# A message-passing layer on one core: groups of small units are formed in two periods instead of four or more, the first with 16 tiles instead of 48

## The chip, the cores and the metric

The kernel runs on one core of a Trainium2 chip. The metric is the device time of one execution in microseconds; the span in a profile, from the first to the last instruction, is a little shorter. Engines are named as in the profile: PE multiplies matrices, DVE and ACT work element by element, POOL issues the indirect transfers (gathers and scatters by a list of indices), SP issues the plain ones.

## The reference

A graph has 12500 nodes with 64 features and 800000 edges with 16 attributes, a source and a destination each. Every edge gets a message from both its nodes' features and its attributes; the messages are summed at their destination, and the nodes are updated:

```python
m_in = jnp.concatenate([x[src], x[dst], e_attr], axis=-1)
msg = _silu(m_in @ w_msg)
agg = _segment_sum(msg, dst, N)
return _silu(jnp.concatenate([x, agg], axis=-1) @ w_upd)
```

Sources and destinations are drawn at random, so the edges come in no order.

## The kernel before, in words

**What is computed where.** The product of the concatenation with the weights is split. `tables` (L214) computes each node's part as a source into a table in HBM, `A_d`, and its part as a destination into `BW`, kept on the chip. Of an edge there is then left: take the row of its source from the table, add the part of its destination and of its attributes, apply silu, and add the result to the sum of its destination. Destinations lie in 128 buckets of 98 nodes. Within a tile of 128 edges that all belong to one bucket, destinations can be handled as a one-hot matrix of 98 columns, by products on PE.

**Two halves.** The first half sorts edges into buckets, in a store `st` in HBM; the second takes sorted tiles from the store and computes messages. Both run interleaved.

The first half works in *steps* of 8 tiles (`class Step`, L377; 782 of them). `onehot` (ACT, L394 and L395) marks each edge's bucket, `sums` (L397) and `count` (PE, L421 to L424) count the edges of each bucket, `ranks` (DVE, L429) finds each edge's place in its bucket, `expand` (DVE, L442) puts its record (16 attributes, and source and destination in one number) at that place, `move` (PE, L459) brings the records to their bucket's row. After 8 or 12 tiles the row block is copied (ACT, L464), the buckets' pointers are advanced (`place`, L477 and L478), and POOL scatters the block to the store (`scatter`, L482). The first 140 chunks have 8 tiles, so nearly every one of these steps scatters; later chunks have 12, so two steps in three do. The steps read segments of indices (`seg_load`, 9 steps each) and edge attributes (`ea_load`, L243, 3 steps each) by plain transfers that SP issues; `records` (ACT at L272) reads the attributes one period after they were asked for.

The second half works in *batches* of up to 8 tiles (`class Batch`, L616): `gather` (POOL, L645, one instruction for each tile), `onehot` (DVE at L655, ACT at L656), `transpose` (PE at L664, ACT at L667), `product` (PE, L673), `message` (DVE at L677, ACT at L678), `reduce` (PE, L694), `add` (DVE, L706). There are 818 batches with 6322 gathers.

**Groups.** Batches belong to *groups* (`class Group`, L489). A group is a list of units of `u` tiles that are taken from the buckets as far as these are filled. The kernel begins with units of one tile (64 tiles in all, in batches of 8), goes on with units of two (640 tiles in groups of 24 and batches of 6), and then has units of four in groups of 64 (`FIRST`, L37, and `QU`). Forming a group takes several stages, numbered by `g.k`, one for each period:

- 0: *bounds*. Five small DVE operations (L540 to L545) count each bucket's new units, a product on PE with a triangular matrix (L577) sums them up over the buckets. Its result lies in the PSUM buffer with the tag `ag`, which `reduce` uses too; there is one such buffer.
- 1: *matrix*. Nine DVE operations (L548 to L558) make from it a matrix that says which unit comes from which bucket; three products on PE (L581 to L583) turn it into a list.
- 2 and on: *loads*. DVE writes the list as integers (`rows`, L588 and L589), SP reads it and issues one transfer for each unit (L564) from the store to one of four buffers `rt`. `NL` (L39) says how many a period has: 16 units of one tile, 8 of two, 8 of four. The transfers wait for the last scatter that was issued when the bounds were computed (L570).
- `g.t0`: *indices*. DVE converts the sources to integers, `sidx` (L525), and the destinations to `lo` (L526, L527). Only two groups may be past this point and not yet used up.

`g.t0` is 2 plus the number of periods with loads. After stage `t0` the group is ready, and the next period may take its first batch.

**The order.** It is written out by hand: `period` (L711) emits, for every engine, one piece of each stage of both halves. Each engine executes its own instructions strictly in this order. A step passes through its stages in successive periods (one-hot and sums; count, ranks and expansion; move; scatter), and so does a batch: gather in the first, transposes and product in the second, message in the third, reduction and addition in the fourth. Formation stages come in two places: `fourth` (DVE) near the start of the period, behind the batch's one-hot, and `middle` (PE) and `fifth` (DVE) at its end.

**The planner.** Whether a group may start is decided when the program is built, without the data. `Draws` (L768) fills 16 sets of buckets with random numbers of a fixed seed, and a group starts when all 16 hold enough (`holds`, L799), when the stage has tiles left (`size`, L817), and when no other group is at an earlier stage of its formation (`may_start`, L852). So the program, and with it the period in which each group starts, is fixed. `step` (L858) is one period with a step; 782 of them are followed by the periods that empty the store.

Of the kernel before, what the change touches and what calls it, by code (L numbers as in the profile page):

```python
# [3 lines left out]
F32 = mybir.dt.float32  # L4
# [3 lines left out]
OP = mybir.AluOpType  # L8
# [6 lines left out]
P = 128  # L15
NBK = 128
BK = 98
# [5 lines left out]
M = 8  # L23
# [3 lines left out]
S = LIM[-1]  # L27
# [6 lines left out]
QU = 4  # L34
# [1 line left out]

FIRST = [(1, 48, BT, (1, 0, 1, 0)), (2, 24, 6, (3, 3, 2, 2))]  # L37
DUM = GT
NL = {1: 16, 2: 8, QU: 8}  # L39
ZB = M // 2  # L40
RK = float(C * P)
SEG = 9 * M
# [6 lines left out]
def mpnn_kernel(tc, x, e_attr, src, dst, w_msg, w_upd, out):  # L49
    nc = tc.nc  # L50
# [22 lines left out]
    with es:  # L73
# [46 lines left out]


        cb = pc.tile([P, 512], F32, name="cb")
        ioB = cb[:, 0:P]
        ioS = cb[:, P:P + S]
        hit = cb[:, 2 * P:2 * P + M * S].rearrange("p (k s) -> p k s", s=S)
        nc.vector.tensor_copy(ioB, iof)
        nc.vector.tensor_scalar(out=ioS, in0=iof[:, 0:S], scalar1=RK, scalar2=None, op0=OP.add)


# [359 lines left out]
        class Group:  # L489


            def __init__(g, u, ptr, done_old, done_new, ceil, gt=GT, base=None, cap=None, bt=BT):
                g.u, g.ptr, g.done_old, g.done_new, g.ceil, g.gt = u, ptr, done_old, done_new, ceil, gt
                g.base = ub[u] if base is None else base
                g.b0, g.cap = None, cap
                g.gu, g.bt = gt // u, bt
                g.nl = NL[u]
                g.t0 = 2 + (g.gu + g.nl - 1) // g.nl
                g.k = 0
                g.over = False  # L500
                g.rt = RT[state["rt"]]
                state["rt"] = (state["rt"] + 1) % len(RT)
# [27 lines left out]
            def fourth(g):  # L530
                k = g.k
                gu = g.gu
                if k == 0:
                    urec = g.u * P
                    c = (urec - 1) / (2.0 * urec) * (1.0 if g.ceil else -1.0)
                    g.blocks = len(blocks)
                    wl = wp.tile([NBK, 8], F32, name="wl")
                    g.wl = [wl[:, i:i + 1] for i in range(8)]
                    a1, v, new, e0, s, e, t1, cbc = g.wl
                    nc.vector.scalar_tensor_tensor(out=a1, in0=g.ptr, scalar=1.0 / urec, in1=g.base, op0=OP.mult, op1=OP.subtract)  # L540
                    nc.vector.tensor_scalar(out=v, in0=a1, scalar1=c, scalar2=MAGIC, op0=OP.add, op1=OP.add)
                    if g.cap is not None:
                        nc.vector.tensor_tensor(out=v, in0=v, in1=g.cap, op=OP.min)
                    nc.vector.scalar_tensor_tensor(out=new, in0=v, scalar=-MAGIC, in1=g.done_old, op0=OP.add, op1=OP.subtract)
                    nc.vector.tensor_tensor(out=t1, in0=g.base, in1=g.done_old, op=OP.add)  # L545
                elif k == 1:
                    a1, v, new, e0, s, e, t1, cbc = g.wl
                    nc.vector.tensor_tensor(out=e0, in0=g.ps[:, 0:1], in1=new, op=OP.add)  # L548
                    nc.vector.tensor_scalar(out=s, in0=g.ps[:, 0:1], scalar1=float(gu), scalar2=None, op0=OP.min)  # L549
                    nc.vector.tensor_scalar(out=e, in0=e0, scalar1=float(gu), scalar2=None, op0=OP.min)  # L550
                    g.mat = mat = wp.tile([NBK, GT], F32, name="mat")
                    nc.vector.tensor_scalar(out=mat[:, 0:gu], in0=iof[:, 0:gu], scalar1=s, scalar2=None, op0=OP.is_ge)

                    nc.vector.tensor_tensor(out=t1, in0=t1, in1=s, op=OP.subtract)
                    nc.vector.tensor_tensor(out=a1, in0=e, in1=s, op=OP.subtract)
                    nc.vector.scalar_tensor_tensor(out=mat[:, 0:gu], in0=iof[:, 0:gu], scalar=e, in1=mat[:, 0:gu], op0=OP.is_lt, op1=OP.mult)
                    nc.vector.tensor_scalar(out=cbc, in0=t1, scalar1=float(g.u), scalar2=-float(D0), op0=OP.mult, op1=OP.add)
                    nc.vector.tensor_tensor(out=g.done_new, in0=g.done_old, in1=a1, op=OP.add)  # L558
                elif k < g.t0:
                    if k == 2:  # L560
                        g.rows()
                    for u in range((k - 2) * g.nl, min(gu, (k - 1) * g.nl), 8):
                        for i, t in enumerate(regs(g.row, u, min(8, gu - u), ENG.SP, TOP - g.u)):
                            j = nc.sync.dma_start(g.rt[:, (u + i) * g.u:(u + i + 1) * g.u, :].rearrange("p a c -> p (a c)"),  # L564
                                                  st_t[ds(t, g.u), :].rearrange("t (q f) -> (t q) f", f=g.u * R))
                            tc.add_to_no_dep_group("units", j.ins)
                            if len(blocks) > g.blocks:
                                for b in blocks[g.blocks:]:
                                    tc.declare_no_dep(j.ins, b, reason=WHOLE)
                                tc.add_manual_dep(j.ins, blocks[g.blocks - 1].name, mybir.DependencyInfo(mybir.DependencyClass.Sync, mybir.DependencyReason.DATA), reason=WHOLE)  # L570

            def middle(g):

                gu = g.gu
                if g.k == 0:
                    g.ps = pag.tile([P, 512], F32, name="ps1", tag="ag")
                    nc.tensor.matmul(g.ps[:, 0:1], tri, g.wl[2], start=True, stop=True)  # L577
                elif g.k == 1:
                    cbc, mat = g.wl[7], g.mat
                    g.ps = pag.tile([P, 512], F32, name="ps2", tag="ag")  # L580
# [35 lines left out]
        class Batch:  # L616
# [35 lines left out]
            def onehot(t):  # L652
                i0, n = t.i0, t.n
                t.q = qp.tile([P, BT, KQ], F32, name="q")
                nc.vector.tensor_tensor(out=t.q[:, 0:n, 0:BK], in0=ioB[:, None, 0:BK].to_broadcast([P, n, BK]), in1=t.grp.lo[:, i0:i0 + n, None].to_broadcast([P, n, BK]), op=OP.is_equal)  # L655
# [55 lines left out]
        def period(step=None, batch=None, ptr_new=None):  # L711
# [17 lines left out]
                g.fourth()  # L729
            if z:  # L730
                z.count()
            if t:
                t.transpose(0)
                t.weights()
                t.transpose(1)
# [12 lines left out]
                z.expand()  # L748
            if h and not early:
                h.sums()  # L750
            if p:
                e = p.move(0)
            if t:
# [62 lines left out]

        def size():  # L817
            g = stages[state["stage"]]
            return g["gt"] if g["total"] is None else min(g["gt"], g["total"] - state["taken"])

        work = dict(cur=None, forming=[], b=0, used=0)

# [35 lines left out]
        def step():  # L858
# [5 lines left out]
            if pipe["z"] and pipe["z"].last:  # L864
                if flow["npl"] % 64 == 0:
                    flow["ptrs"] = sg.tile([NBK, 64], I32, name="ptrs")
                pn = flow["ptrs"][:, flow["npl"] % 64:flow["npl"] % 64 + 1]
                flow["npl"] += 1
            b = take()
            if size() and may_start() and draws.holds(state["u"], size() // state["u"]):  # L870
                draws.take(state["u"], size() // state["u"])
# [11 lines left out]
            next(tab)  # L883
        while flow["ic"] < len(steps) or pipe["h"] or pipe["z"]:
            step()
            for _ in range(4 if flow["ic"] < 5 else 1):
                next(tab, None)
            if zeros and flow["ic"] > 1:
                later()
# [285 lines left out]
```

## Time and profile before

| what | us |
|---|---|
| median of three runs | 8929.77 |
| lowest and highest | 8925.74 and 8931.5 |
| the profiled execution | 8929.85 |
| its span, first to last instruction | 8928.0 |
| last gather issued | 8906.46 |

The page of the profile gives each engine's busy time with its share of the span; a group of instructions has a line, an engine, an operation, the tile that it writes and those that it reads, the number, the busy time and mean duration, and the idle time of the engine just before them with what ended it. In the timeline the first column is the start and the second the duration, both in us; brackets at the end hold the idle time of the engine before the instruction, and who ended it. SPq and POOLq are the queues of an engine that issues transfers.

### The profile page before, as it was taken

The page shows a single profiled execution, that of the slowest core. Times are in us where ns is not written, and L with a number is a line of the kernel's source. Part 1 is how long each engine was busy: PE and PEld are TensorE (multiplying, and loading weights), DVE is VectorE, ACT ScalarE, POOL GpSimd, SP SyncE. Part 2 cuts the span into 40 slices and gives each one's busy share as a digit, 9 for nine tenths or more (in the row PEclk, how much of TensorE's full clock was granted, in tenths as well). Part 3 has the DMA queues.
Part 4 walks back from the last instruction along what each step waited for, and adds up shares of the span by engine and source line. Part 5 has one row for each costly group of instructions (what it writes and reads, how often), then busy time and mean ns, then how long its engine had stood idle before and what let it go on. Part 6 is the DMA issues. An engine that isn't in the chain of part 4 may idle for free. (4 is left out here: it accounts for less than half of the span.)

```text
span 8928.0 us, 155380 instructions
## 1 busy us (share of the span) xinstructions
PE 8156.2 (91%) x49053; PEld 5873.2 (66%) x49816; DVE 7216.6 (81%) x15722; ACT 5054.3 (57%) x12594; POOL 6599.6 (74%) x6908
## 2 busy tenths in 40 slices
PE   8899999999999999999999999999999999999767
PEld 5677776666666666666666666666666666666656
DVE  8999998888888888888888888888888888887233
ACT  7666666555555555555555555555555555555222
POOL 1677777777777777777777777777777777777776
PEclk9999999999999999999999999999999999999566
DMA  4222222222222222222222222222222222222323
GB/s 109 56 62 60 60 61 58 50 57 54 54 56 50 57 52 56 52 56 52 56 52 56 56 52 52 55 57 52 56 52 56 52 56 55 52 57 49 59 48 51
DMA packets 662901, 501.14 MB, mean 56 GB/s; under 512 B 492983, under 2 KB 529911, under 8 KB 662071
## 3 DMA queue, kind: packets, MB, share of 16 engines
q0 software_dynamic: 238976, 349.72, 16.8%
q1 hardware_dynamic: 422775, 141.27, 7.3%
q8 instruction: 401, 6.57, 0.3%
q14 instruction: 429, 3.51, 0.1%
q10 hardware_dynamic: 320, 0.07, 0.0%
HBM read 330.05 MB, written 152.30 MB: 54 GB/s over the span
## 5 line engine op out<-in xcount | busy, mean ns | idle before, releaser
L645 POOL DMA_INDIRECT g<-A_d,sidx x6322 | 6020.1, 952 | 1946.6 <-issue 1546.2
L459 PE MATMUL pl<-X,hf 128*128 128x291 f32 (+5 forms) x12512 | 4255.3, 492 | 6.2 <-DVE LOST L477 6.2
L459 PEld LDWEIGHTS pl<-X,hf 128*128 128x128 f32 x12512 | 2389.5, 198 | 1333.1 <-issue 842.5
L442 DVE TENSOR_TENSOR X<-cb,rec 128x442 f32<-128x442 f32 (+5 forms) x3128 | 2646.9, 908 | 26.7
L394 ACT ACTIVATE hf<-iof,shi 128x128 f32<-128x128 f32 x6256 | 1908.3, 389 | 872.9 <-PE pl L459 872.6
L673 PEld LDWEIGHTS pre<-w,qt 114*128 114x128 f32 x10496 | 1338.1, 202 | 580.7 <-issue 562.8
L673 PE MATMUL pre<-w,qt 114*128 114x64 f32 x10496 | 1343.6, 284 | 249.0 <-DVE g L677 247.3
L677 DVE TENSOR_TENSOR g<-pre,g 128x512 f32<-128x512 f32 (+1 forms) x818 | 548.9, 671 | 1191.7 <-DMA g<-A_d,sidx 769.4
L678 ACT ACTIVATE g<-g 128x512 f32<-128x512 f32 (+1 forms) x818 | 501.6, 613 | 1761.5 <-DVE g L677 1759.7
L694 PE MATMUL ag<-q,g 128*64 128x98 f32 x12644 | 775.8, 264 | 250.4 <-DVE wl L549 146.1
L429 DVE TENSOR_REDUCE rank<-z 128x8 f32<-128x1024 f32 x782 | 949.1, 1214 | 57.3 <-PE z L424 36.3
L395 ACT ACTIVATE hf<-hf,ones 128x1024 f32<-128x1024 f32 x782 | 899.1, 1150 | 25.4
L667 ACT ACTIVATE qt<-tq 114x1024 f32<-114x1024 f32 (+1 forms) x818 | 797.2, 975 | 156.5 <-PE tq L664 154.2
L664 PE MATMUL tq<-ident,q 128*114 128x128 f32 x6322 | 871.5, 283 | 14.3 <-ACT nodes L194 13.0
L694 PEld LDWEIGHTS ag<-q,g 128*64 128x64 f32 x12644 | 613.3, 143 | 411.5 <-issue 200.6
L664 PEld LDWEIGHTS tq<-ident,q 128*114 128x114 f32 x6322 | 766.9, 140 | 136.5 <-ACT nodes L194 20.5
L482 POOL DMA_INDIRECT st<-blk,ptrs x567 | 572.9, 1010 | 321.2 <-issue 141.1
L655 DVE TENSOR_TENSOR q<-cb,lo 128x784 f32<-128x784 f32 (+1 forms) x818 | 767.4, 938 | 2.2
L464 ACT ACTIVATE blk<-pl 128x512 f32<-128x512 f32 (+1 forms) x568 | 323.8, 570 | 782.9 <-PE pl L459 609.7
L706 DVE TENSOR_TENSOR ACC<-ag,ACC 64x98 f32 x1938 | 497.5, 257 | 108.6 <-PE ag L694 28.8
L422 PE MATMUL z<-G,onesb 128*128 128x384 bf16 x1564 | 511.4, 327 | 73.5 <-DVE G L403 13.7
L673 PE MATMUL pre<-BW,qt 114*128 (+1 forms) x2148 | 311.8, 305 | 109.4 <-DVE g L677 108.6
(137 smaller groups left out, 5099.1 us busy)
## 6 DMA issues: line engine op xcount, KB each, us to landing
g<-A_d,sidx POOLq DMA_INDIRECT x6322
ea<-in_e_attr SPq DMA_DIRECT2D x260, 192.0 KB
rt<-st SPq DMA_DIRECT2D x1312, 34.0 KB
st<-blk,ptrs POOLq DMA_INDIRECT x567
rt<-st SPq DMA_DIRECT2D x434, 8.5 KB
nodes<-in_x SPq DMA_DIRECT2D x62, 98.0 KB
ACC<-rt SPq DMA_DIRECT2D x11, 544.0 KB
rt<-st SPq DMA_DIRECT2D x320, 17.0 KB
```

Source lines behind the costliest of these rows:

```text
L394: nc.scalar.activation(c.hf[:, k, :], iof, AF.Square, bias=c.hi[:, k:k + 1])
L395: nc.scalar.activation(c.hf, c.hf, AF.Relu, bias=ones, scale=-1.0)
L429: nc.vector.tensor_reduce(out=c.rank, in_=c.z, axis=AX.X, op=OP.max)
L442: nc.vector.tensor_tensor(out=c.x[:, k:k + 2, 2:2 + n * R].rearrange("p k (s c) -> p k s c", c=R), in0=hit[:, k:k + 2, 0:n, None].to_broad ...
L459: nc.tensor.matmul(pl[:, 0:w], c.hf[:, k, :], c.x[:, k, 0:w], start=(n == (c.size - 1 if whole else 0)), stop=ends, skip_group_check=True)
L482: i = nc.gpsimd.indirect_dma_start(out=st, out_offset=bass.IndirectOffsetOnAxis(ap=c.ptr, axis=0), in_=c.blk[:, 2:], in_offset=None)
L645: j = nc.gpsimd.indirect_dma_start(out=t.g[:, i, :], out_offset=None, in_=A_d, in_offset=bass.IndirectOffsetOnAxis(ap=t.grp.sidx[:, k:k + ...
L655: nc.vector.tensor_tensor(out=t.q[:, 0:n, 0:BK], in0=ioB[:, None, 0:BK].to_broadcast([P, n, BK]), in1=t.grp.lo[:, i0:i0 + n, None].to_broa ...
L664: nc.tensor.transpose(t.tq[0:KQ, j * P:(j + 1) * P], t.q[:, j, :], ident)
L667: nc.scalar.activation(t.qt[:, 0:w], t.tq[0:KQ, 0:w], AF.Copy)
L673: nc.tensor.matmul(t.pre[:, i * D:(i + 1) * D], t.qt[:, i * P:(i + 1) * P], w, start=True, stop=True)
L694: o = nc.tensor.matmul(t.ag[t.half(v), v // 2 * BK:(v // 2 + 1) * BK], t.g[:, i, :], t.q[:, i, 0:BK], start=(k == 0), stop=(k == u - 1))
```

## The change

Four things change.

- **Formation of groups of one- and two-tile units** (those with a cap, `quick`). Bounds and matrix fall into one period: the product of the bounds is emitted right behind `count`, the matrix behind `expand` and `sums`, its three products at the period's end. All loads fall into the next period: `NL[2]` becomes 12, and `g.nl` is the whole group. `g.t0` still counts the periods by `NL`, 16 units each for one-tile units: 3 for the first group and for groups of two-tile units, 5 for the group of 48. The indices are made at the beginning of the period that follows, ahead of `take`, so that this same period can take the first batch.
- **The first group** has 16 tiles instead of 48; the second has the other 48.
- **The bounds' product** is written to one column of the constants' PSUM buffer `cb`, for every group, no longer to the buffer that `reduce` uses. The constants are narrowed for it.
- **The tables** are advanced twice in every fourth period instead of once in each.

Groups of four-tile units keep their stages.

```diff
-NL = {1: 16, 2: 8, QU: 8}
+NL = {1: 16, 2: 12, QU: 8}
...
-        ioB = cb[:, 0:P]
-        ioS = cb[:, P:P + S]
-        hit = cb[:, 2 * P:2 * P + M * S].rearrange("p (k s) -> p k s", s=S)
-        nc.vector.tensor_copy(ioB, iof)
+        ioB = cb[:, 0:BK]
+        ioS = cb[:, BK:BK + S]
+        hit = cb[:, P:P + M * S].rearrange("p (k s) -> p k s", s=S)
+        nc.vector.tensor_copy(ioB, iof[:, 0:BK])
+        ps1 = cb[:, 2 * P + M * S:2 * P + M * S + 1]
...
-                g.nl = NL[u]
-                g.t0 = 2 + (g.gu + g.nl - 1) // g.nl
+                g.quick = cap is not None
+                g.nl = g.gu if g.quick else NL[u]
+                g.t0 = 2 + (g.gu + NL[u] - 1) // NL[u]
...
-                    nc.vector.tensor_tensor(out=e0, in0=g.ps[:, 0:1], in1=new, op=OP.add)
-                    nc.vector.tensor_scalar(out=s, in0=g.ps[:, 0:1], scalar1=float(gu), scalar2=None, op0=OP.min)
+                    nc.vector.tensor_tensor(out=e0, in0=ps1, in1=new, op=OP.add)
+                    nc.vector.tensor_scalar(out=s, in0=ps1, scalar1=float(gu), scalar2=None, op0=OP.min)
...
-                    g.ps = pag.tile([P, 512], F32, name="ps1", tag="ag")
-                    nc.tensor.matmul(g.ps[:, 0:1], tri, g.wl[2], start=True, stop=True)
+                    nc.tensor.matmul(ps1, tri, g.wl[2], start=True, stop=True)
...
             if z:
                 z.count()
+            quick = [g for g in forms if g.quick and g.k == 0]
+            for g in quick:
+                g.middle()
+                g.k = 1
...
             if h and not early:
                 h.sums()
+            for g in quick:
+                g.fourth()
...
-            return g["gt"] if g["total"] is None else min(g["gt"], g["total"] - state["taken"])
+            if g["total"] is None:
+                return g["gt"]
+            return NL[1] if not state["stage"] and not state["taken"] else min(g["gt"], g["total"] - state["taken"])
...
+            for g in work["forming"]:
+                if g.quick and g.k == g.t0:
+                    g.fifth()
             b = take()
...
-            for _ in range(4 if flow["ic"] < 5 else 1):
+            for _ in range(4 if flow["ic"] < 5 else 1 + (flow["ic"] % 4 == 1)):
                 next(tab, None)
```

More of the change, by code (lines that the diff above doesn't have):

```diff
@@ L654, in onehot @@
                 t.q = qp.tile([P, BT, KQ], F32, name="q")
-                nc.vector.tensor_tensor(out=t.q[:, 0:n, 0:BK], in0=ioB[:, None, 0:BK].to_broadcast([P, n, BK]), in1=t.grp.lo[:, i0:i0 + n, None].to_broadcast([P, n, BK]), op=OP.is_equal)
+                nc.vector.tensor_tensor(out=t.q[:, 0:n, 0:BK], in0=ioB[:, None, :].to_broadcast([P, n, BK]), in1=t.grp.lo[:, i0:i0 + n, None].to_broadcast([P, n, BK]), op=OP.is_equal)
                 nc.scalar.activation(t.q[:, 0:n, BK:KQ], t.grp.rt[:, i0:i0 + n, 0:DE], AF.Copy)
```

## The prediction

> **What bounds the kernel now.** I read the page's busy line, then the groups and waits of POOL alone, then the timeline around the first batches, the only place with holes.
>
> ```profile
> PE 8156.2 (91%) x49053; PEld 5873.2 (66%) x49816; DVE 7216.6 (81%) x15722; ACT 5054.3 (57%) x12594; POOL 6599.6 (74%) x6908
> ```
>
> By shares PE looks like the limit. The groups of POOL between 329 and 8906 us say otherwise (columns: busy, mean ns, idle before):
>
> ```profile
> L645 POOL DMA_INDIRECT g<-A_d,sidx x6257 | 5958.5, 952 | 1913.8 <-issue 1530.0 <-DMA g<-A_d,sidx 232.6 <-PE ag L694 52.4
> L482 POOL DMA_INDIRECT st<-blk,ptrs x532 | 538.0, 1011 | 162.2 <-issue 139.0 <-ACT G L401 5.5 <-ACT qt L667 4.6
> L983 POOL DMA_INDIRECT st<-X,pe x4 | 3.9, 973 | 8.2 <-issue 5.6 <-DVE ACC L706 2.6
> ```
>
> The waits of POOL in the same window (total, times, longest):
>
> ```profile
> POOL g L645 <- issue: 1530.0, 5021, 0.3
> POOL g L645 <- PE z L424: 9.5, 8, 7.4
> ```
>
> Busy plus idle is 8585 us, the whole window, and no gather waits longer than 0.3 us but the one at its left edge. So a gather takes POOL (5958.5 + 1913.8 - 7.4)/6257 = 1.257 us and a scatter (538.0 + 162.2)/532 = 1.316, and POOL issues them without a break. From 329 us on, the kernel is as long as POOL's list; other engines wait for it. Its one hole lies before:
>
> ```profile
> 293.22 0.94 POOL L645 DMA_INDIRECT g<-A_d,sidx  x1 [0.30 <-DVE LOST L477]
> ...
> 328.84 0.97 POOL L645 DMA_INDIRECT g<-A_d,sidx  x1 [7.36 <-PE z L424]
> ```
>
> Between these, POOL only had the scatters of five periods without a batch. The sum is therefore not "what does PE save" but "when does POOL start for good, and with how much left".
>
> **The planner's periods.** Lines 768 to 879 draw from a fixed seed, so which period starts which group follows from their rules alone; I went through them period by period, counted from 0. Before: 852 periods, 782 of them with a step, 818 batches (the trace has 782 of L429, 818 of L677). First group starts in 20, its batches run 26 to 33, 34 to 38 are empty, two-tile batches begin in 39. After: the 16-unit group starts in 18, batches in 20 and 21; the 48-unit group starts in 23, batches 27 to 32; 33 to 35 are empty; two-tile batches begin in 36. The list is the same 818 batches. Later the store holds no more than before, and period 391 has no batch; 850 periods in all. So the lead is three periods at 36 and two at the end. As POOL is the limit, what counts is the time of the first gather of period 36 (after) against 328.84 (period 39 before): both have 6258 gathers behind them.
>
> **The start, worked through.**
>
> ```profile
> 156.32 0.16 DVE L540 SCALAR_TENSOR_TENSOR wl<-ptrs,ub 128x1 f32<-128x1 int32 x1
> ...
> 157.11 1.22 DVE L429 TENSOR_REDUCE rank<-z 128x8 f32<-128x1024 f32 x1
> ...
> 163.25 0.15 DVE L548 TENSOR_TENSOR wl<-ps,wl 128x1 f32<-128x1 f32 x1
> ...
> 164.11 1.22 DVE L429 TENSOR_REDUCE rank<-z 128x8 f32<-128x1024 f32 x1
> ```
>
> Bounds cost DVE 0.8 us (156.32 to 157.11), matrix 0.9 (163.25 to 164.11). Loads, as SP issues them, and what waits for them:
>
> ```profile
> 171.53 9.12 SPq L564 DMA_DIRECT2D rt<-st  x16
> ...
> 182.36 18.88 SPq L564 DMA_DIRECT2D rt<-st  x32
> 201.28 0.43 SPq L243 DMA_DIRECT2D ea<-in_e_attr  x1
> ```
>
> ```profile
> 202.93 0.22 DVE L525 CAST sidx<-rt 128x64 int32<-128x64 f32 x1 [5.71 <-DMA rt<-st]
> ...
> 203.42 0.97 POOL L645 DMA_INDIRECT g<-A_d,sidx  x1 [13.35 <-DVE sidx L525]
> ...
> 203.77 0.52 ACT L272 ACTIVATE rec<-ea 128x384 f32<-128x384 f32 x1 [8.32 <-DVE slo L146]
> ...
> 208.97 0.16 DVE L438 TENSOR_TENSOR X<-rank,limc 128x8 f32<-128x8 f32 x1
> ```
>
> A load costs SP 18.88/32 = 0.59 us, the last lands 1.7 us after its issue (201.24 to 202.93), and DVE already stood 5.71 us for it. Periods without and with a full batch:
>
> ```profile
> 107.64 1.03 PE L198 MATMUL abp<-wab,nodes 128*98 128x256 f32 x4
> ```
>
> ```profile
> 143.43 1.22 DVE L429 TENSOR_REDUCE rank<-z 128x8 f32<-128x1024 f32 x1 [0.38 <-PE z L424]
> ...
> 150.04 1.23 DVE L429 TENSOR_REDUCE rank<-z 128x8 f32<-128x1024 f32 x1 [0.38 <-PE z L424]
> ```
>
> ```profile
> 229.61 1.21 DVE L429 TENSOR_REDUCE rank<-z 128x8 f32<-128x1024 f32 x1
> ...
> 239.53 1.21 DVE L429 TENSOR_REDUCE rank<-z 128x8 f32<-128x1024 f32 x1
> ```
>
> 6.6 us bare, 9.9 with a batch in every stage.
>
> - Four extra turns of the tables (1.0 us of PE in the row, about 1.3 with its transposes) fall into periods where PE has no room: between 0 and 5 us, I take 3, as most of it should show.
> - Ranks of period 18: 143.4 + 3 = 146.4, with bounds 146.8. Period 19: + 6.6 + 0.9 = 154.4. SP starts some 0.8 after the ranks, as before (171.53, behind ranks at 164.11 + 6.6), 155.2; 16 loads take 9.1, landing 1.7: conversion at 166.0, **first gather at 166.5, 37 us earlier.** DVE stands there some 5 us again, and behind the conversion on its queue stand one-hot, ranks and expansion, for which PE and then the scatters wait; POOL has nothing else to do then.
> - Periods 20 to 24, from ranks at 167.6 (conversion and one-hot behind 166.0): 7.5, 6.6, 7.7 and 10.2, estimates between the bare and the full period by the stages that hold a batch, with the second group's bounds and matrix: its rows at 199.5. SP then issues **48 loads in one go**: 200.4 + 48 x 0.59 = 228.7.
> - Queued behind them on SP is period 25's load of edge attributes, which period 26 reads on ACT (L272). In 201.28 to 203.77 it took at most 2.5 us: ACT's record starts at about 231.2, where without the queue period 26 would be there at some 210. From there to the end of the sums is 5.2 us (203.77 to 208.97), pointer 0.4, conversion 0.5: **period 27's first gather at 237.5.** If the attributes did not hold it, the loads' own landing (230.4) would: 231; if neither, the program's own 221 (199.6 + 8.5 + 7.0 + 5.9, again by the stages).
> - Six batches at POOL's pace. Eight took 203.42 to 294.16, 11.34 each: 68.0, so 305.5.
>
> What follows the last of these gathers is shown by the hole of before:
>
> ```profile
> 296.13 0.67 DVE L677 TENSOR_TENSOR g<-pre,g 128x512 f32<-128x512 f32 x1
> ...
> 304.87 1.20 DVE L429 TENSOR_REDUCE rank<-z 128x8 f32<-128x1024 f32 x1
> ...
> 313.13 0.22 DVE L478 SCALAR_TENSOR_TENSOR ptrs<-blk,LOST,ptrs 128x1 int32<-128x1 f32 x1
> ...
> 327.85 0.21 DVE L525 CAST sidx<-rt 128x64 int32<-128x64 f32 x1 [0.15 <-issue]
> ```
>
> ```profile
> 305.67 3.96 SPq L564 DMA_DIRECT2D rt<-st  x8
> ...
> 310.63 1.88 SPq L564 DMA_DIRECT2D rt<-st  x4
> ```
>
> - Message 2.0 us after the gather (294.16 to 296.13): 307.5. To the next ranks 8.7 and, new here, matrix, rows and a segment's preparation, 1.8: 318.0. Rows there; 12 loads (0.8 + 5.8) and the landing end at 326.3. DVE arrives 8.5 us after the ranks (304.87 to 313.35) at 326.5: no further wait. Gather 1.0 after the conversion (327.85 to 328.84): **period 36 starts at 327.5, against 328.84: -1.3 us.**
> - But it starts three periods earlier in the steps, and each of these still has a scatter for POOL: + 3 x 1.316 = +3.9.
> - Empty period 391: POOL is a batch and more behind the program by then, so the conversion comes before it is needed. Between 0 and one POOL period (8 x 1.257 + 2/3 x 1.316 = 10.9); I take 0.5, since its list runs on.
> - From then on a quick group's loads are asked for one period after its bounds, and wait for the scatter issued with these (L570). POOL is 7.1 us behind DVE there (rival 3): four gathers and the scatter, 6.3, and a landing of some 2 put it 15.4 us after the one-hot, the rows 9.8 after it. SP stands 5.6 us, issues 5.8 of loads by 21.2; an attribute load behind them is due on ACT three periods after the start, some 26. Cover of 2 to 3 us: nothing.
> - The bounds' result moves out of the shared bank: the wait of PE's reduction (below) goes. POOL covers it: nothing. Narrower views of the constants: nothing.
>
> **Sum:** -1.3 + 3.9 + 0.5 = +3 on this execution's 8929.85 (span 8928.0), which lies 0.1 above the median of three: **8933 us.** Bounds of this case: all loads hidden (gather at 221, -16.5) gives 8916; tables at 5 and a whole period lost at 391 give 8933 + 2 + 10.4 = 8945.
>
> **Rivals.**
>
> ```profile
> PE ag L694 <- DVE wl L549: 146.1, 86, 4.8
> ```
>
> ```profile
> L645 POOL DMA_INDIRECT g<-A_d,sidx x481 | 453.9, 944 | 146.5 <-issue 133.4 <-DMA g<-A_d,sidx 6.7 <-PE ag L694 1.8
> ```
>
> 1. *PE is the bound.* Then the wait of the reduction for L549 is the prize: 146 us, 8784. For it: 91% and the row. Against: POOL's unbroken list. Chance 0.05.
> 2. *DVE is the bound.* Then only the count of periods matters: two fewer at the end, where a batch takes 8 x (453.9 + 146.5)/481 = 10.0 us (second row, 8300 to 8900 us): -20, 8910. Against: in that very stretch POOL has no gap over 0.3 us. Chance 0.08. [...] The trace disagrees: POOL's idle comes in 0.3 us pieces that no other engine ends.
> 3. *Slower: the quick groups starve POOL in the two-tile stage.* The second half of the forming now sits at the end of the same period on PE, behind a matrix that DVE makes after its expansion:
>
> ```profile
> 420.12 0.76 DVE L655 TENSOR_TENSOR q<-cb,lo 128x588 f32<-128x588 f32 x1
> ...
> 425.48 3.01 DVE L442 TENSOR_TENSOR X<-cb,rec 128x442 f32<-128x442 f32 x4
> ...
> 428.07 0.34 PE L577 MATMUL ps<-wl,tri 128*128 128x1 f32 x2
> ...
> 430.69 0.89 PE L694 MATMUL ag<-q,g 128*64 128x98 f32 x12 [0.62 <-DVE wl L549]
> ```
>
> ```profile
> 427.22 0.95 POOL L645 DMA_INDIRECT g<-A_d,sidx  x1 [0.30 <-PE pl L459]
> ```
>
> PE would be done at 428.07, the matrix would come at 428.49 + 0.86: 1.3 us of PE per group, queued before the next period's counts, ranks, X and so scatters. 29 groups: 37 us. Cover: POOL reaches a batch 7.1 us after DVE's one-hot (420.12 to 427.22). If nothing is won back between groups, it is used up after six, and the rest costs 37 - 7 = 30: 8963. Against: the wait of 0.62 goes, and DVE needs the same work in all. Chance 0.17.
>
> **Chances.** Forecast 0.70, rivals 0.05, 0.08, 0.17. Below 0.2% (18 us, about what a measurement of this kernel can tell from no change) lies the forecast; faster are 1 and 2, slower is 3. Range 8908 to 8964: the forecast's bounds, rival 2 and rival 3's price; it leaves out PE and the far sides, under 0.2.
>
> **What would show it.** First gather near 166; a run of 48 loads on SP near 200 to 229 with ACT's L272 standing for the attributes behind it; first gather of period 27 near 237; the last start of POOL near 328; then no gap on POOL beyond 0.3 us but at L983. Waits of the reduction for L549 gone, total unmoved. Wrong: gaps on POOL in 330 to 1250 (rival 3), or a list that ends with POOL idle while others work (1, 2).

## The result, and the profile after

| | us |
|---|---|
| before, median of 6 runs | 8929.59 (8925.74 to 8932.23) |
| after, median of 6 runs | 8971.86 (8969.94 to 8973.89) |
| ratio after to before | 1.0046, 95% interval 1.0036 to 1.0056 |
| span of the profiled execution after | 8971.5 |

The kernel became slower by 42 us; 8933 was forecast, with 8908 to 8964 as the range. The line numbers named here are one or two higher in the kernel after than in that of before: L566 are the loads and L527 the conversion to indices (two higher), L646 is the gather, L695 the reduction, L578 the bounds' product, L582 to L584 the matrix's three products (one higher).

The page's busy line, the counterpart of the first line that the prediction shows:

```profile
PE 8199.8 (91%) x49055; PEld 5905.1 (66%) x49816; DVE 7237.0 (81%) x15722; ACT 5059.0 (56%) x12594; POOL 6592.9 (73%) x6908
```

It says nothing of the loss. The start does, in the timeline (start, duration, idle before in brackets):

```profile
154.53 9.54 SPq L566 DMA_DIRECT2D rt<-st  x16
...
165.66 0.22 DVE L527 CAST sidx<-rt 128x64 int32<-128x64 f32 x1 [5.41 <-DMA rt<-st]
...
166.15 0.97 POOL L646 DMA_INDIRECT g<-A_d,sidx  x1 [12.03 <-DVE sidx L527]
...
201.53 27.95 SPq L566 DMA_DIRECT2D rt<-st  x48
...
232.09 0.52 ACT L273 ACTIVATE rec<-ea 128x384 f32<-128x384 f32 x1 [15.96 <-DMA ea<-in_e_attr]
...
238.33 0.97 POOL L646 DMA_INDIRECT g<-A_d,sidx  x1 [20.97 <-DVE sidx L527]
...
305.08 0.94 POOL L646 DMA_INDIRECT g<-A_d,sidx  x1 [0.30 <-issue]
...
330.36 0.97 POOL L646 DMA_INDIRECT g<-A_d,sidx  x1 [15.17 <-DVE lo L529]
...
1323.87 0.96 POOL L646 DMA_INDIRECT g<-A_d,sidx  x1 [0.31 <-issue]
...
8949.26 0.94 POOL L646 DMA_INDIRECT g<-A_d,sidx  x1 [0.30 <-issue]
```

The gather at 330.36 is the first of the two-tile stage, the one at 1323.87 the first behind it, the last is POOL's last. The kernel before has the first at 328.84, the last at 8906.46, and between them:

```profile
1280.66 0.96 POOL L645 DMA_INDIRECT g<-A_d,sidx  x1 [0.30 <-PE tq L664]
```

So the two-tile stage took 951.8 us before and 993.5 after. Of the 42.8 us by which the last gather comes later, 1.5 are lost at the start, 41.7 in this stage, and behind it 0.4 are won. Inside the stage POOL has stopped being the limit. Its waits from 360 to 1210 us, before and then after (total, times, longest):

```profile
POOL g L645 <- issue: 127.7, 419, 0.3
POOL g L645 <- DMA g<-A_d,sidx: 27.4, 90, 0.3
```

```profile
POOL g L646 <- PE ag L695: 30.0, 22, 3.5
POOL st L483 <- ACT blk L465: 22.5, 31, 2.0
```

Before, no wait of POOL in this stretch was over 0.3 us; waits of 3.5 and 2.0 us for other engines are new. And PE's waits in the same stretch, before and after:

```profile
PE ag L694 <- DVE wl L549: 32.5, 24, 2.5
PE ag L694 <- PE tq L664: 3.5, 8, 1.0
```

```profile
PE cb L578 <- DVE wl L546: 44.9, 24, 4.0
PE ps L582 <- DVE wl L559: 5.8, 14, 0.5
```

One wait per group was replaced by another: PE, having finished count, stands for the bounds, 1.87 us each time. With the waits at the matrix, PE's waits grow by only 0.6 us a group ((44.9 + 5.8 - 32.5 - 3.5)/24). What else there is shows in the granted clock. The stretch 360 to 1210 us by the windows view, before and after (busy us of PE, PEld, DVE, ACT, POOL; granted clock; DMA share; GB/s):

```profile
360.00:1210.00 850.00, 806.73 (x4959) 607.62 (x5055) 806.54 (x2142) 548.61 (x1367) 647.01 (x667) 0.99 0.26 61
```

```profile
360.00:1210.00 850.00, 792.99 (x4736) 592.53 (x4825) 769.46 (x2054) 523.27 (x1304) 614.07 (x636) 0.96 0.25 59
```

One such place in small windows, and PE's timeline there:

```profile
976.00:978.00 2.00, 1.24 (x7) 0.54 (x7) 1.46 (x7) 1.97 (x8) 1.68 (x2) 1.00 0.18 33
978.00:980.00 2.00, 0.97 (x5) 0.98 (x6) 1.90 (x7) 1.26 (x2) 1.39 (x3) 0.79 0.30 104
980.00:982.00 2.00, 2.00 (x16) 1.66 (x15) 0.64 (x2) 1.08 (x2) 0.77 (x1) 0.50 0.18 33
982.00:984.00 2.00, 2.00 (x8) 1.15 (x7) 1.48 (x5) 0.44 (x2) 1.04 (x2) 0.86 0.00 0
984.00:986.00 2.00, 2.00 (x9) 1.39 (x8) 1.93 (x6) 0.00 (x0) 1.70 (x2) 1.00 0.17 33
```

```profile
976.93 0.38 PE L425 MATMUL z<-G,onesb 128*128 128x512 bf16 x1
979.03 0.48 PE L578 MATMUL cb<-wl,tri 128*128 128x1 f32 x2 [1.72 <-DVE wl L546]
979.37 1.51 PE L665 MATMUL tq<-ident,q 128*114 128x128 f32 x6
...
988.60 0.20 PE L582 MATMUL ps<-mat,wl 128*1 128x12 f32 x2 [0.31 <-DVE wl L559]
...
989.84 0.82 PE L665 MATMUL tq<-ident,q 128*114 128x128 f32 x6
```

PE waits 1.72 us, and from about 979.2 to 982.5 it is granted half its clock: the same six transposes take 1.51 us at 979.37 and 0.82 at 989.84. The reduction comes late, DVE stands for it in `add`, and POOL for the buffer that the reduction frees:

```profile
982.42 0.83 DVE L707 TENSOR_TENSOR ACC<-ag,ACC 64x98 f32 x3 [1.78 <-PE ag L695]
...
982.65 0.94 POOL L646 DMA_INDIRECT g<-A_d,sidx  x1 [1.89 <-PE ag L695]
```

The clock records of both traces hold two values, 1.0 and 0.5; the shortest stretch at 0.5 in either is 3.41 us. From 330 to 1250 us the kernel before has 6 stretches at 0.5, 20.5 us in all; after has 17, 81.9 us. As an estimate from these times and the six transposes (1.51 us against 0.82), the 61.4 us more at half the clock can cost PE about half of them, 31 of the 41.7 us.

### The profile page after: what moved, and what is told of

Same layout as the page of the kernel before. It is cut to its first block, busy times and chain, and to the rows that moved or that the text cites. A ratio compares the mean times of both kernels' runs of the same rounds, so it can differ in the third digit from the quotient of the medians.

```text
span 8971.5 us, 155447 instructions
## 1 busy us (share of the span) xinstructions
PE 8199.8 (91%) x49055; PEld 5905.1 (66%) x49816; DVE 7237.0 (81%) x15722; ACT 5059.0 (56%) x12594; POOL 6592.9 (73%) x6908
## 5 line engine op out<-in xcount | busy, mean ns | idle before, releaser
L646 POOL DMA_INDIRECT g<-A_d,sidx x6322 | 6019.8, 952 | 2002.2 <-issue 1561.9
L443 DVE TENSOR_TENSOR X<-cb,rec 128x442 f32<-128x442 f32 (+5 forms) x3128 | 2647.2, 909 | 26.7
L674 PE MATMUL pre<-w,qt 114*128 114x64 f32 x10496 | 1322.3, 282 | 236.2 <-DVE g L678 235.0
L665 PE MATMUL tq<-ident,q 128*114 128x128 f32 x6322 | 909.9, 291 | 14.4 <-ACT nodes L195 12.9
L665 PEld LDWEIGHTS tq<-ident,q 128*114 128x114 f32 x6322 | 802.9, 145 | 142.3 <-ACT nodes L195 20.4
L695 PE MATMUL ag<-q,g 128*64 128x98 f32 x12644 | 783.5, 265 | 24.7 <-PE tq L665 11.8
L695 PEld LDWEIGHTS ag<-q,g 128*64 128x64 f32 x12644 | 620.3, 144 | 184.3 <-issue 138.8
```

What stands on the lines that cost most here:

```text
L443: nc.vector.tensor_tensor(out=c.x[:, k:k + 2, 2:2 + n * R].rearrange("p k (s c) -> p k s c", c=R), in0=hit[:, k:k + 2, 0:n, None].to_broad ...
L646: j = nc.gpsimd.indirect_dma_start(out=t.g[:, i, :], out_offset=None, in_=A_d, in_offset=bass.IndirectOffsetOnAxis(ap=t.grp.sidx[:, k:k + ...
L665: nc.tensor.transpose(t.tq[0:KQ, j * P:(j + 1) * P], t.q[:, j, :], ident)
L674: nc.tensor.matmul(t.pre[:, i * D:(i + 1) * D], t.qt[:, i * P:(i + 1) * P], w, start=True, stop=True)
L695: o = nc.tensor.matmul(t.ag[t.half(v), v // 2 * BK:(v // 2 + 1) * BK], t.g[:, i, :], t.q[:, i, 0:BK], start=(k == 0), stop=(k == u - 1))
```

## The experiments

Times are medians; each ratio is to the kernel before on the same chip (8930.5 to 8931.1 in the three sets; 8929.59 for after). The stage is the two-tile stage from its first gather to the first behind it; half clock is what the records show from 330 to 1250 us. These two columns come from one profiled execution each. Those of gap, matrix_next and one_go took 8974.4, 8989.58 and 8936.74 us, 13 to 17 more than their medians; what they took longer lies behind the stage (7639 to 7647 us from its end to the last gather, against 7624 to 7629 in the others), so the stages can be compared.

| kernel | us | ratio to before, interval | stage, us | half clock: stretches, us |
|---|---|---|---|---|
| before | 8930.5 | | 951.8 | 6, 20.5 |
| after | 8971.86 | 1.0046, 1.0036 to 1.0056 | 993.5 | 17, 81.9 |
| column_only | 8927.98 | 0.9998, 0.9989 to 1.0007 | 951.4 | 4, 13.7 |
| early_place_only | 8930.37 | 1.0001, 0.9991 to 1.0010 | 954.6 | 3, 17.1 |
| late_bounds | 8963.56 | 1.0038, 1.0023 to 1.0054 | 980.8 | 18, 61.4 |
| attributes_ahead | 8960.08 | 1.0034, 1.0021 to 1.0047 | 986.7 | 17, 64.8 |
| gap | 8957.69 | 1.0029, 1.0018 to 1.0041 | 974.1 | 10, 44.4 |
| matrix_next | 8976.67 | 1.0051, 1.0037 to 1.0065 | 985.9 | 18, 68.3 |
| one_go | 8919.77 | 0.9988, 0.9979 to 0.9997 | 950.9 | 3, 10.2 |
| sixteens_best | 8969.62 | 1.0044, 1.0030 to 1.0057 | 985.8 | 17, 68.3 |
| fill | 8948.25 | 1.0020, 1.0011 to 1.0029 | 970.8 | 4, 17.1 |
| covered | 8934.88 | 1.0005, 0.9996 to 1.0014 | 953.7 | 8, 34.1 |
| two_covered | 8913.85 | 0.9982, 0.9973 to 0.9991 | 957.9 | 6, 23.9 |
| one_go_early | 8940.96 | 1.0011, 1.0002 to 1.0020 | 970.4 | 17, 58.0 |

### First set: which wait, and what the parts cost alone

**late_bounds**: the bounds' product behind the reduction.

```diff
             quick = [g for g in forms if g.quick and g.k == 0]
-            for g in quick:
-                g.middle()
-                g.k = 1
...
             if r:
                 r.reduce()
+            for g in quick:
+                g.middle()
+                g.k = 1
```

> The changed kernel, with the product of a quick group's bounds emitted behind the reduction instead of behind the count on PE; all else as changed. Theory A (PE stands about 1.9 us per two-tile group for DVE's bounds, in front of transposes and reduction, and the late reduction holds DVE's addition and POOL's buffers): the small gaps of POOL between 370 and 1215 us go, about 40 us, so 8930 to 8936 us. Theory B (bounds, matrix and indices now lie in neighbouring stretches of DVE, and DVE is what is short of time): unchanged, 8968 to 8974. Theory D (the two-tile stage starts without the lead that POOL's backlog gave before, whatever the order on PE): most of it stays, 8955 to 8970.

Measured 8963.56, not theory A's 8930 to 8936. But theory A is not tested by it: the wait did not go, it moved to where the prediction's third rival had put it, and both waits together hardly shrank (48.4 us against 50.7):

```profile
PE ps L582 <- DVE wl L559: 36.9, 24, 1.7
PE cb L578 <- DVE wl L546: 11.5, 21, 2.6
```

The time lies in theory D's range (the lead lost at the start). Against D stands covered, in the third set: its stage starts as late as that of after (330.19 against 330.36) and keeps only 1.9 us of the loss.

**column_only** (the kernel before, the bounds' result in `cb`'s column) and **early_place_only** (that, and the bounds' product behind count; matrix and loads in the periods of before):

```diff
-                    g.ps = pag.tile([P, 512], F32, name="ps1", tag="ag")
-                    nc.tensor.matmul(g.ps[:, 0:1], tri, g.wl[2], start=True, stop=True)
+                    nc.tensor.matmul(ps1, tri, g.wl[2], start=True, stop=True)
```

```diff
                 z.count()
+            for g in forms:
+                if g.cap is not None and g.k == 0:
+                    g.middle()
```

> The kernel before, with the one part that the bounds' product goes to a column of the constants' buffer instead of the buffer of the reduction; groups formed as before. If POOL's list is the limit, the reduction's wait for L549 (146 us in all before) goes and the time stays: 8922 to 8936 us. If PE is the limit: towards 8784. If the shared buffer of the constants makes DVE's one-hot wait for PE in a way that counts: above 8945.

> The kernel before, with the column and with the bounds' product of one- and two-tile groups behind the count on PE; matrix, loads and indices in the periods of before, groups of 48 and 16. Theory A: PE stands for the bounds here too (0.9 us at the median by the rows of before, as the conversion of indices lies in another period), POOL has its backlog of 7 us to use up first: 0 to 20 us more, 8930 to 8950, with the wait of PE for L544 in the profile. Theory B: unchanged, 8930. Theory D: unchanged, 8930, since the backlog of the start is that of before.

Neither moves the time. In column_only the reduction's wait for L549 is gone, as forecast, but PE did not win it. The bounds' product now waits instead, for the expansion on DVE, which reads the buffer that the product writes:

```profile
PE cb L577 <- DVE X L443: 20.5, 22, 2.3
```

All of PE's waits from 360 to 1210 us are 37.0 us in before and 35.8 here; from 329 to 8906 us, 141.3 us for L549 became 178.1 for L443. So this run doesn't show what PE would win without the wait. The early place costs nothing by itself, and there the wait is short:

```profile
PE cb L577 <- DVE wl L545: 23.5, 23, 3.1
```

That is 1.0 us each time against 1.87 in the kernel after, and 3 stretches at half clock instead of 17.

**attributes_ahead**: edge attributes asked for one period earlier.

```diff
-            if eo >= M:
+            if eo >= 0:
                 load_ea(e0 + EAT)
```

> The changed kernel, with each load of edge attributes asked for one period earlier, so that in period 24 it stands on SP ahead of the 48 loads and not behind them. If ACT's record of period 26 was held by it, the first gather of period 27 comes at about 231 instead of 238.3 (then held by the loads themselves), and that of period 36 some 7 us earlier; the total falls by as much at most, 8962 to 8972, as the two-tile stage behind it is not POOL's any more. If the loads alone held it: no move of that gather.

Period 27's first gather came at 230.35 instead of 238.33, so the edge attributes behind the 48 loads did hold it, as the prediction had it (231 without). The total, 8960.08, is just under the 8962 to 8972 expected: the stage starts 7.7 us earlier and is 6.8 us shorter. It keeps 34.9 of its 41.7 us of loss (986.7), so the lead lost at the start is not the main cause.

### Second set: parts of the forming pulled apart

**gap** (no start in the period behind a conversion), **matrix_next** (two-tile groups: matrix one period later), **one_go** (the kernel before with 12 loads in one period), **sixteens_best** (matrix_next, attributes_ahead and four groups of 16). Of each, in this order, the lines that are new in it:

```diff
                     live.append(g)
+                    work["gap"] = True
...
-            if size() and may_start() and draws.holds(state["u"], size() // state["u"]):
+            if not work.pop("gap", False) and size() and may_start() and draws.holds(state["u"], size() // state["u"]):
```

```diff
             for g in quick:
                 g.middle()
-                g.k = 1
+                g.k = 1 if g.u == 1 else 0
+            quick = [g for g in quick if g.u == 1]
+            wait = [g for g in forms if g.quick and g.k == 0]
...
             for g in forms:
-                g.middle()
+                if g not in wait:
+                    g.middle()
                 g.fifth()
```

```diff
-NL = {1: 16, 2: 8, QU: 8}
+NL = {1: 16, 2: 12, QU: 8}
```

```diff
-FIRST = [(1, 48, BT, (1, 0, 1, 0)), (2, 24, 6, (3, 3, 2, 2))]
+FIRST = [(1, 16, BT, (1, 0, 1, 0)), (2, 24, 6, (3, 3, 2, 2))]
```

> The kernel after, but a new group may not start in the period that follows a conversion (L527) of the group before it: its bounds come one period later. Batches, empty periods and 850 periods in all stay as they were. In the kernel after, the two-tile stage goes at 9.3 to 9.4 us a period, POOL's list alone would go at 8.9, and a cycle of four periods reads 8.3, 8.3, 9.8 (conversion ahead of the ranks) and 10.8 (bounds, waiting products, matrix). Theory of lumps (DVE's conversion, bounds and matrix stand within one period; PE has no work stored for it, so what one period has too much the next can't give back): conversion apart from bounds and matrix gives about half of the loss back, 8945 to 8958. Theory of the two waits of PE (it waits for the bounds and for the matrix in one period): nothing changes in that period, 8966 to 8976. Theory of loads in one go (12 loads of a group asked for in one period): nothing changes, 8966 to 8976.

> The kernel after, but for groups of two-tile units the matrix and its three products stand in the period behind the bounds again, at the places of before; the bounds' product stays behind count, all loads stay in one period, the next. Two-tile batches begin in period 37 instead of 36, period 391 has a batch, 850 periods as before. Cost of the later start on POOL: a period of some 7.5 us, less one scatter of 1.3, so +6 without a cure. Theories of lumps and of the two waits in one period both expect the cure: the two-tile stage back at POOL's pace of 8.9 us a period, the 41 us gone, 8937 to 8948 in all. Theory of loads in one go: no cure, 8970 to 8985. If only the lead lost at the start counted: 8970 to 8980.

> The kernel before, with one thing of the change: 12 loads of a two-tile group in one period instead of 8 and 4. Two-tile batches begin in period 38 instead of 39, 851 periods. Theory of loads in one go: the two-tile stage goes at 9.3 us a period, 8955 to 8975. All others: loads cost nothing, and the stage starts a bare period (7 us) earlier less one scatter (1.3): 8921 to 8931.

> matrix_next, and the one-tile stage in four groups of 16 instead of 16 and 48, so that batches run through periods 20 to 27 and no queue of 48 loads forms; edge attributes are asked for one period earlier. Two-tile batches begin in period 37. Theories of lumps and of the two waits: the ranks of period 28 come at about 245 to 250 us, nine bare periods of 7 to 7.4 later is period 37, so first two-tile gather near 312 to 320, 20 us before matrix_next: 8915 to 8930, under before's 8930 at the low end. If the two-tile stage isn't cured by the later matrix: 8945 to 8970.

gap lands at the upper edge of what the theory of lumps gives it, with PE's wait for the bounds hardly shorter (1.72 us each time), but with 10 stretches at half clock instead of 17:

```profile
PE cb L579 <- DVE wl L547: 42.9, 25, 3.7
```

matrix_next speaks against it and against that of the two waits in one period: with the matrix a whole period away nothing is cured. The wait for the bounds is there, and longer:

```profile
PE cb L578 <- DVE wl L546: 53.3, 25, 6.1
```

one_go rules out the loads: alone they cost nothing and bring the stage forward by a period, to 8919.77, below the kernel before. sixteens_best, built on matrix_next, kept the loss, and missed its own forecast for the start as well: its first two-tile gather came at 330.2, not at 312 to 320. A likely reason, not tested, is that batches that run earlier lengthen the periods in which they run (6.6 us bare against 9.9 with a batch, in the prediction), so that the program reaches that gather no sooner.

What did sort the ten kernels so far was the last column of the table: stage and half clock grow together. That alone doesn't say which is the cause; it became the theory of the third set.

### Third set: wait or clock

**fill**: four products more on PE ahead of count, in the periods in which a two-tile group forms; count overwrites their result.

```diff
             if z:
+                if any(g.quick and g.k == 0 and g.u == 2 for g in forms):
+                    z.fill()
                 z.count()
...
+            def fill(c):
...
+                for a in range(4):
+                    k = a % 2 * ZB
+                    nc.tensor.matmul(c.z[:, k:k + ZB, :], w1, hb[:, k:k + ZB, :], start=True, stop=True)
```

**covered**: bounds' product behind the transposes, matrix behind add.

```diff
                 t.transpose(1)
+            for g in quick:
+                g.middle()
+                g.k = 1
             if r:
                 r.reduce()
...
                 r.add()
+            for g in quick:
+                g.fourth()
```

**two_covered**: the start of before, with one-tile groups formed as before, and covered's way for two-tile groups. Of its lines, the one that keeps one-tile groups as before:

```diff
-                g.quick = cap is not None
+                g.quick = cap is not None and u == 2
```

**one_go_early**: one_go and early_place_only together, each of which costs nothing alone.

> The kernel after, with more work for PE: in each period that forms a two-tile group, four products of 512 columns (0.39 us each, 1.6 in all) ahead of count, into the bank that count then overwrites; the output stays the reference's. PE executes them in the time in which it would wait for the bounds (1.9 us, 24 times). Clock theory: what costs is not the wait but the half clock that the records show behind it (granted clock 0.50 in stretches of 3.4 us, 17 of them and 81.9 us from 330 to 1250 us, against 6 and 20.5 in the kernel before). With PE busy instead of idle these stretches go, and more work makes the kernel faster: at most 8 of them, two-tile stage 960 to 972 us (after 993.5, before 951.8, first gather of the stage to first gather behind it), 8938 to 8955 in all. Theory of the wait alone (time is lost in which PE does nothing useful): no change, 8966 to 8978.

> The kernel after, bounds and matrix still in one period, at other places: the bounds' product behind the batch's transposes, so that these cover it, and the matrix behind add, ahead of sums and expansion, so that it is there before PE's three products at the period's end. Clock theory, and theory of the wait: no wait of PE over 1.2 us, at most 6 stretches at half clock, two-tile stage 951 to 960 us, 8928 to 8940 in all (the start of after, 1.5 us behind before and with more scatters left, stays). Theory of lumps on DVE (conversion, bounds and matrix of 3 us within one period, wherever PE's products stand): 8955 to 8972.

> The start of before (48 tiles, then 16, with one-tile groups formed as before, tables as before), and covered's way for two-tile groups alone: their batches begin in period 36 instead of 39. Clock theory: first two-tile gather at 310 to 316 instead of 328.8, three scatters of 1.3 still to do, the stage at POOL's pace: 8912 to 8926, the fastest so far but perhaps for the kernel with loads in one go (8919.8). Theory of lumps: 8945 to 8960.

> The kernel before with 12 loads in one go (8919.8 by itself) and the bounds' product behind count, in the column (8930.4 by itself, against 8930.5): neither alone costs anything. Together they put conversion and the next group's bounds next to each other on DVE with PE waiting behind them. Clock theory: waits of PE of 1.6 us and more, some 24 of them, 12 or more stretches at half clock, 8940 to 8962. Theory of the wait alone: 24 times about 0.8 us more than the wait for L549 that it replaces, 19 us less the cover, 8922 to 8938. If neither matters without the rest of the change: 8916 to 8923.

All four times fell where the clock theory had them, one_go_early at the very edge, 3 us above what the wait alone was given. For covered the theory of the wait had the same range, so fill and one_go_early are the runs that tell the two apart. The theory of lumps on DVE falls with covered and two_covered, for which it had 8955 and 8945 at least. In fill the four products began at 961.91 and count 0.91 us later, less than the 1.6 us that were meant, since these products followed each other at 0.23 us; so a shorter wait remained:

```profile
PE cb L586 <- DVE wl L554: 25.1, 22, 3.9
PE ps L590 <- DVE wl L567: 9.4, 23, 0.4
```

```profile
961.91 1.06 PE L433 MATMUL z<-hf,w 128*128 128x512 bf16 x4
962.82 0.39 PE L423 MATMUL z<-hf,w 128*128 128x512 bf16 x1
...
964.77 0.38 PE L586 MATMUL cb<-wl,tri 128*128 128x1 f32 x2 [0.80 <-DVE wl L554]
965.01 0.85 PE L673 MATMUL tq<-ident,q 128*114 128x128 f32 x6
```

```profile
360.00:1210.00 850.00, 814.90 (x5052) 599.66 (x5050) 789.36 (x2099) 536.71 (x1336) 633.26 (x653) 1.00 0.26 61
```

Wait and useless work together take PE 1.14 + 0.91 us at the bounds, more than the 1.87 of after. But the transposes behind them take 0.85, not 1.51, the clock of the stretch is 1.00 instead of 0.96, and the kernel takes 23.6 us less with more to do (1.0020 of before instead of 1.0046). That is the wait apart from the clock: of the 41.7 us that the stage had lost, at least 22.7 (993.5 to 970.8) go with the half clock. The 19.0 that fill still loses (970.8 to 951.8) lie with PE's time without use, to which fill's own products add 0.91 us a group; so how much of the 41.7 the wait alone costs in after is not shown.

covered takes most of both away, and the stage is back at 953.7. Its forecast of no wait over 1.2 us was wrong: PE still waits 1.4 us at the bounds, but with 8 stretches at half clock, two more than forecast and 9 fewer than after.

```profile
PE cb L578 <- DVE wl L546: 30.6, 22, 3.5
```

one_go and one_go_early are the smallest pair: 21 us by the place of one product (and its column, which costs nothing in column_only).

```profile
PE cb L577 <- DVE wl L545: 40.8, 24, 2.6
```

1.70 us each time, 17 stretches at half clock. And two_covered, which keeps the three periods that the change wins and loses only 6.1 us in the stage (957.9, one more scatter among them), is the fastest: first two-tile gather at 307.4, earlier than the 310 to 316 expected and 21 us before that of the kernel before, 8913.85 in all, 0.9982 of before and 58 us under the kernel after. one_go, a change of one number, is at 0.9988; the intervals of the two overlap.

## Why the prediction was wrong

- **POOL as the limit, and the start: right.** First gather 166.15 (166.5 forecast), 48 loads end at 229.5 (228.7), the attributes hold ACT until 232.09 (231.2), period 27 begins at 238.33 (237.5), the last one-tile gather ends at 306.02 (305.5). Only the two-tile stage began 2.9 us later than forecast, 330.36: the message behind that gather came at 309.23, not 307.5, and the next ranks at 320.30, not 318.0.
- **Three scatters more, and period 391: right, but the price of the scatters doesn't show.** POOL's groups from 330.4 us on have 535 scatters for 532:

```profile
L483 POOL DMA_INDIRECT st<-blk,ptrs x535 | 535.0, 1000 | 178.2 <-issue 147.5 <-ACT blk L465 24.8 <-ACT hf L395 1.5
```

  One of the three lies in the stage. From the first gather behind the two-tile stage to the last, 7625.4 us after and 7625.8 before, with two scatters more: the empty period costs nothing, and of the 3.9 us put down for scatters these two show none.
- **The reduction's wait for L549 goes, the total stays: right in number** (column_only), but the prediction did not see that PE's wait comes back at the bounds' product, so it isn't a test of rival 1, PE as the limit of the whole. What speaks against rival 1 is the stretch behind the stage: there one_go_early stands at half clock for 1088.8 us and before for 968.1, and both take the same time (7625.4 and 7625.8 us). Rival 2, DVE, falls too: covered has the same 850 periods as after and isn't below before.
- **The step that failed** is the one on the forming from period 36 on, which weighed only the loads of a quick group and put "nothing". PE's product of the bounds, moved from the period's end, where PE had other work in front of it, to behind count, got no price at all. Rival 3 did price a wait of PE, 1.3 us a group at the end of the period, and gave 8963 for it; the chance was 0.17. Measured, the wait at the end is 0.24 us a group (5.8 in 24) and the one in the middle 1.87. So the loss is rival 3's in kind (the program falls behind POOL in this stage, POOL then shows gaps) but not at its place, and at least 22.7 of its 41.7 us go with something that no rival had, the half clock behind the waits (17 stretches in after, 4 in fill).
- **Why the cover did not hold** is argued from one row, not tested. POOL's 7.1 us behind DVE are a stock that is used up once, as rival 3 had it. What the stage can bear each time is its room, and the windows row of before shows how little that is: PE 806.73 and DVE 806.54 us busy of 850, some 43 us each over 24 groups, 1.8 us a group, of which PE spent 1.35 waiting for L549 already. The argument against rival 3, that a wait of 0.62 goes and DVE has the same work in all, weighed one group's rows and not this room.
- A reading of the prediction that is too strong: that no other engine ends POOL's pieces of 0.3 us. In the row it shows, 151 of 1913.8 us are put down to other engines; all but one of these pieces (7.4 us, at the left edge) are of 0.3 us, so POOL's list stands as it was read.
- What stays open: why matrix_next's waits are longer (2.1 us) than after's. That conversion and the next group's bounds stand next to each other on DVE ahead of the product fits one_go_early against early_place_only (1.70 against 1.02 us), and gap, where they stand apart (42.9 us in 25 waits, 1.72), only in part.

## What to carry to other kernels

Where the limit is an engine with no gaps, still price each new wait of the engines behind it, once per round, against the room of that stage (its windows row), not against a lead. In this kernel a wait of PE had a second price, the clock granted behind it: 0.50 behind the wait of 1.72 us at 979.03, where six transposes took 1.51 us instead of 0.82. It counted where PE had no room, in the two-tile stage; behind that stage 121 us more at half clock (one_go_early against before) cost nothing. Where it counts, put the product behind work that PE can do meanwhile, as covered did (stage 953.7 us for 993.5). If the trace shows half-clock stretches behind a wait, giving PE anything to do there is a quick test of which of the two costs, as fill was here (4 stretches for 17, 23.6 us less).

## What the runs showed of the hardware

PE's waits at the bounds' product from 360 to 1210 us, by the waits view of each run, beside the half clock that its records show from 330 to 1250 us:

| kernel | waits: us, times | mean, us | half clock: stretches, us |
|---|---|---|---|
| column_only | 20.5, 22 | 0.93 | 4, 13.7 |
| early_place_only | 23.5, 23 | 1.02 | 3, 17.1 |
| fill | 25.1, 22 | 1.14 | 4, 17.1 |
| covered | 30.6, 22 | 1.39 | 8, 34.1 |
| two_covered | 31.0, 22 | 1.41 | 6, 23.9 |
| one_go_early | 40.8, 24 | 1.70 | 17, 58.0 |
| gap | 42.9, 25 | 1.72 | 10, 44.4 |
| after | 44.9, 24 | 1.87 | 17, 81.9 |
| matrix_next | 53.3, 25 | 2.13 | 18, 68.3 |

late_bounds, whose longer wait is the one at the matrix (36.9 us in 24, 1.54 each, and 11.5 in 21 at the bounds), has 18 stretches and 61.4 us. In before PE waits at the reduction instead (32.5 us in 24, 1.35 each), with 6 stretches and 20.5 us.

This fits the three sets: a mean wait of 1.0 us (early_place_only, 8930.37 against 8930.5) is free, one of 1.4 (covered, 1.9 us in the stage) nearly so, and one of 1.7 (one_go_early) costs 21 us in all. The order of the rows is not strict: gap, with 1.72, has 10 stretches and one_go_early, with 1.70, 17. The means don't say which single waits bring it.
